# Attention's head mix on quarters of TensorE, with regroupings in halves issued from GpSimd

## The chip, the core and the metric

The kernel runs on one core of a Trainium2 chip. A core has five engines with a queue of instructions each: TensorE (PE, an array of 128 x 128 cells for matmuls), VectorE (DVE), ScalarE (ACT), GpSimd (POOL) and SyncE (SP, which only issues DMAs). PE writes to PSUM, a memory of eight banks of 128 partitions x 512 float32; DVE and ACT read the banks, POOL doesn't. The queues run side by side and wait for each other by semaphores; each is worked off in its order. The metric is the device time of one execution in microseconds (us); lower is better.

## What is computed

Three layers follow each other. The first is attention whose heads are mixed before and after the softmax; the change touches this layer alone. B = 4 batches, 12 heads, 448 positions, 64 numbers per head, all in float32:

```python
scores = scale * np.matmul(q, k.transpose(0, 1, 3, 2))
scores = np.einsum('bhij,hg->bgij', scores, w_pre)
scores = scores - np.max(scores, axis=-1, keepdims=True)
attn = np.exp(scores)
attn = attn / (np.sum(attn, axis=-1, keepdims=True) + 1e-09)
attn = np.einsum('bhij,hg->bgij', attn, w_post)
return np.matmul(attn, v).astype(np.float32)
```

Its output goes to a dense layer (`h = x @ w_in`, `g = h * cos(h)`, `g @ w_out`) and to a layer of eight experts; these make up the rest of the program.

## The kernel before, in words

Attention is `phase_a`. A batch's 448 query rows are cut into four tiles of 120, 120, 120 and 90 rows (`ROWS`; the last ones overlap), 16 tiles in all. For each tile:

- `q_prep` turns the tile's queries by transposes on PE (tile name qt) and splits them into a high and a low part (q_hi, q_lo), with the rows sorted by their place in a ten. `k_prep` does it for the keys once a batch (kt, k_hi, k_lo).
- `scores` makes two heads at a time (name s): three products each, the two heads on the upper and the lower half of the array's rows. ACT or DVE copies each head's scores from PSUM to SBUF (ss).
- `sort` regroups: a DMA for each head moves its 120 x 448 scores into the tile s2, where a partition is a pair of one of ten rows and a head (10 x 12 = 120 partitions), and column block c holds the c-th ten of rows. It is issued by SP or by POOL. These are the rows `s<-ss` (for the first tile `s<-am`, since the scores rest in a tile am there).
- `pre` mixes the heads of ten rows by one matmul (name pre): a matrix `kron_pre` of 120 x 120, in which `w_pre` stands once for each of ten rows, times a column block of s2. DVE takes the maximum of each row (`top`, name mz), ACT the exponential and its sum (`exp`, name e). Three such blocks are a group; there are 60 groups and 180 blocks.
- `fin` makes 1/sum and scales the second mixing matrix `kron_post` with it (`weigh`, name wc). `post` then multiplies e with wc (name po): for each of four column parts three matmuls into one bank, copied out to am.
- `av` multiplies am with v: three steps of 16 matmuls a tile, two heads on the left and the right half of the array's columns.

Next to this, `narrow` converts the weights of the dense layer, which lie in DRAM in a wider format: a load (raw), some DVE and ACT operations (cvt, nar), an integer addition on POOL (nar, L542) and a store, 64 times.

The order of all this is made by a planner (`Plan`): each operation has the engines that could do it with a duration, a due time and what it depends on, and `schedule` deals them out one by one. It also counts the buffers (`PLACES`: three PSUM banks for pre, two for post, three for the others). What it settles is written into the queues in that order. `half` says whether a matmul uses the array in halves, and `TURN` is what the planner charges for going over.

## Time and profile before

| | |
|---|---|
| time, median of 3 runs | 934.05 us (928.82 to 935.58) |
| profiled execution | 931.55 us; span of its instructions 929.8 us |
| busy in the span | PE 887.1, DVE 610.5, ACT 546.7, POOL 126.6 us |
| pre-mix on PE (L405) | 360 records (two for each of 180 matmuls), 13.6% of the chain of waits |
| posts on PE (L443) | 1440 records, 15.0% of the chain |
| regroupings | 74 + 18 + 7 issued by POOL, 70 + 18 + 5 by SP |

The profile is one execution, taken by the hardware. Each row tells of a group of instructions: the line, the engine, the operation, output<-input by the program's tile names, and sizes as partitions x elements. A float32 matmul is two records on PE. PE's ends are modelled, since its matmuls are pipelined, so the distance between two starts says more than one duration. "The chain" is the work that ended last, followed back from the end, from each step to what released it. The granted clock (PEclk) is the share of TensorE's full speed that it was given.

### The profile page before, as it was taken

The page shows a single profiled execution, that of the slowest core. Times are in us where ns is not written, and L with a number is a line of the kernel's source. Part 1 is how long each engine was busy: PE and PEld are TensorE (multiplying, and loading weights), DVE is VectorE, ACT ScalarE, POOL GpSimd, SP SyncE. Part 2 cuts the span into 40 slices and gives each one's busy share as a digit, 9 for nine tenths or more (in the row PEclk, how much of TensorE's full clock was granted, in tenths as well). Part 3 has the DMA queues.
Part 4 walks back from the last instruction along what each step waited for, and adds up shares of the span by engine and source line. Part 5 has one row for each costly group of instructions (what it writes and reads, how often), then busy time and mean ns, then how long its engine had stood idle before and what let it go on. Part 6 is the DMA issues. An engine that isn't in the chain of part 4 may idle for free.

```text
span 929.8 us, 17837 instructions
## 1 busy us (share of the span) xinstructions
PE 887.1 (95%) x6602; PEld 634.8 (68%) x6602; DVE 610.5 (66%) x1277; ACT 546.7 (59%) x1199; POOL 126.6 (14%) x184
## 2 busy tenths in 40 slices
PE   7879999999999999999999999999999999999765
PEld 5557777777777777777778777777777787853212
DVE  4658888789888798787654656666756667833003
ACT  5547768677766777676665555565646558622003
POOL 2122233222322122222200000000000000010000
PEclk9989999999999999999999999999999999999768
DMA  8999887998879987887437712354464339889998
GB/s 169 206 193 223 203 235 212 231 226 231 227 201 243 226 237 193 225 210 212 123 119 223 266 54 69 119 204 136 154 203 136 116 109 303 260 335 415 415 377 319
DMA packets 179622, 198.89 MB, mean 214 GB/s; under 512 B 70892, under 2 KB 154578, under 8 KB 179536
## 3 DMA queue, kind: packets, MB, share of 16 engines
q1 hardware_dynamic: 169404, 177.14, 64.3%
q0 software_dynamic: 7520, 19.98, 9.0%
q8 instruction: 52, 0.85, 0.4%
q10 hardware_dynamic: 2612, 0.65, 0.3%
q14 instruction: 34, 0.28, 0.1%
HBM read 135.40 MB, written 23.59 MB: 171 GB/s over the span
## 4 chain that ended last, share of the span: by engine, by line
PE 82%; DMA 11%; ACT 2%; SPq 2%; DVE 1%; issue 1%; ACTq 0%; DVEq 0%
PE po L443 15%; PE pre L405 14%; PE h L705 8%; PE av L467 8%; PE h L706 8%; PE h L708 8%; PE s L358 7%; DMA s<-ss 4%; DMA early<-in_moe_w_dram 3%; PE gt L745 3%; DMA ring<-in_moe_w_dram 2%; DMA cg<-in_moe_w_dram 2%; PE eh L1046 2%; PE lg L754 1%; PE p L817 1%; PE kt L292 1%
## 5 line engine op out<-in xcount | busy, mean ns | idle before, releaser
L443 PEld LDWEIGHTS po<-wc,e 120*112 120x112 f32 x1440 | 172.1, 177 | 60.1 <-issue 44.5
L443 PE MATMUL po<-wc,e 120*112 120x120 f32 x1440 | 183.6, 269 | 0.6 <-ACT am L228 0.6
L405 PE MATMUL pre<-s,kron_pre 120*120 120x448 f32 x360 | 166.2, 549 | 2.1 <-DMA s<-ss 1.7
L408 DVE TENSOR_REDUCE mz<-pre 120x1 f32<-120x448 f32 x180 | 111.3, 621 | 49.5 <-PE pre L405 47.8
L705 PE MATMUL h<-x,wh 128*128 128x512 f32 (+1 forms) x384 | 142.0, 380 | 0.7 <-ACT wh L649 0.7
L706 PE MATMUL h<-x,wh 128*128 128x512 f32 (+1 forms) x384 | 136.1, 364 | 0.0
L228 ACT COPY am<-po 112x360 f32<-112x360 f32 x189 | 87.3, 462 | 69.9 <-PE po L443 67.7
L412 ACT ACTIVATE e<-pre,mz 120x448 f32<-120x448 f32 x180 | 114.9, 639 | 21.1 <-DVE mz L408 19.0
L721 ACT ACTIVATE cg<-h,consts 128x512 f32<-128x512 f32 (+1 forms) x64 | 40.4, 632 | 88.2 <-PE h L708 86.9
L705 PEld LDWEIGHTS h<-x,wh 128*128 128x128 f32 x384 | 72.2, 188 | 24.1 <-ACT cg L721 8.0
L708 PE MATMUL h<-x,wf 128*128 128x512 f32 (+1 forms) x384 | 87.5, 363 | 0.0
L467 PE MATMUL av<-am,v 112*64 112x120 f32 (+1 forms) x1536 | 82.8, 262 | 0.7 <-ACT xst L228 0.7
L378 POOL DMA_DIRECT2D s<-ss x92 | 54.8, 596 | 207.4 <-ACT ss L228 107.3
L467 PEld LDWEIGHTS av<-am,v 112*64 112x64 f32 x1536 | 74.0, 137 | 11.2 <-issue 3.0
L542 POOL TENSOR_TENSOR nar<-nar,cvt 128x384 uint32<-128x384 uint32 x64 | 63.9, 999 | 117.2 <-DVE cvt L533 51.4
L706 PEld LDWEIGHTS h<-x,wh 128*128 128x128 f32 x384 | 72.3, 188 | 10.6
L722 DVE TENSOR_SCALAR cg<-cg 128x512 f32<-128x512 f32 (+1 forms) x64 | 25.1, 393 | 78.0 <-ACT cg L721 77.5
L708 PEld LDWEIGHTS h<-x,wf 128*128 128x128 f32 x384 | 66.2, 188 | 11.9
L228 ACT COPY ss<-s 120x448 f32<-120x448 f32 (+1 forms) x102 | 53.1, 532 | 27.9 <-PE s L358 12.5
L650 DVE TENSOR_TENSOR wf<-wf,wh 128x768 fp32r<-128x768 f32 x64 | 60.9, 952 | 11.1 <-ACT wh L649 11.1
L405 PEld LDWEIGHTS pre<-s,kron_pre 120*120 120x120 f32 x360 | 53.0, 184 | 15.5 <-issue 12.5
L226 DVE COPY ss<-s 120x448 f32<-120x448 f32 (+1 forms) x78 | 48.3, 620 | 18.9 <-PE s L358 17.8
(174 smaller groups left out, 1259.6 us busy)
## 6 DMA issues: line engine op xcount, KB each, us to landing
early<-in_moe_w_dram SPq DMA_DIRECT2D x36, 768.0 KB
wf<-w SPq DMA_DIRECT2D x64, 384.0 KB
s<-ss POOLq DMA_DIRECT2D x74, 210.0 KB, 6.4
s<-ss SPq DMA_DIRECT2D x70, 210.0 KB
raw<-in_moe_w_in_dram SPq DMA_DIRECT2D x32, 384.0 KB
w<-nar SPq DMA_DIRECT2D x64, 192.0 KB
raw<-in_moe_w_out_dram SPq DMA_DIRECT2D x32, 384.0 KB
gn<-in_moe_w_dram SPq DMA_DIRECT2D x16, 768.0 KB
```

Of the source, the lines that this page charges most:

```text
L228: nc.scalar.copy(out=out, in_=in_)
L358: nc.tensor.matmul(pts[o][:n, :S], x[r, p, :n], y[r, p, :], start=(i == 0), stop=(i == 2))
L405: nc.tensor.matmul(prt[gi, c][:, :S], kpre, s2t[ti][:, 3 * g + c, :], start=True, stop=True)
L408: nc.vector.tensor_reduce(out=mz[gi][:, 0, c:c + 1], in_=prt[gi, c][:, :S], axis=AX.X, op=ALU.max, negate=True)
L412: nc.scalar.activation(out=et[gi][:, c, :], in_=prt.pop((gi, c))[:, :S], func=AF.Exp, bias=mz[gi][:, 0, c:c + 1], accum_out=mz[gi][:, 1, c ...
L443: nc.tensor.matmul(pt[:, :360].rearrange("p (g i) -> p g i", i=30)[:, :, 10 * c:10 * c + 10], et[gi][:, c, jt * CJ:(jt + 1) * CJ], wct[gi] ...
L467: nc.tensor.matmul(pt[64 * o:64 * o + 64, x * 120:x * 120 + n], vt[:, g, jt, :], am[ti % 2][:, g, jt, :n], start=(jt == 0), stop=(jt == NJ ...
L542: nc.gpsimd.tensor_tensor(out=f, in0=f, in1=x["t"], op=ALU.add)
L650: nc.vector.tensor_tensor(out=wf_t[v], in0=wf_t[v].bitcast(F32), in1=wh.bitcast(F32), op=ALU.subtract)
L705: nc.tensor.matmul(pt, wh[:, c], xh[:, c, :], start=(c == 0), stop=False)
L706: nc.tensor.matmul(pt, wh[:, c], xl[:, c, :], start=False, stop=False)
L708: nc.tensor.matmul(pt, wl[:, c], xh[:, c, :], start=False, stop=(c == 5))
```

## The change

The pre-mix is done on quarters of the array. Query rows are grouped by five instead of ten, so a tile has 24 fives (20 for the last tile, which now has 100 rows instead of 90). s2 has 128 partitions: five rows x 12 heads from partition 0, and another five x 12 from partition 64 (r = 0, 1). `kron_pre` is 60 x 60 (in 64 columns), once in each half of the partitions. A step of `pre` is four matmuls: upper or lower half of the rows (r), left or right half of the columns (c), each with its own column block of s2. They fill two PSUM banks (one for each r) with 2 x 60 rows in 128 partitions. There are 92 such steps, in 44 groups of two and 4 groups of one; DVE takes 184 maxima and ACT 184 exponentials, over 128 partitions. A group's post has four matmuls (two in the groups of one) for each of four column parts, and its copy to am moves 480 columns (240).

`fin` is two operations for the planner, sum and reciprocal (`turn`) and the scaling (`weigh`), both on DVE as before.

Each head's regrouping is two DMAs of half its rows. For all tiles but the first they can be issued by POOL only; for the first by SP or POOL.

The buffers for e go from 3 of three blocks to 5 of two, mz gets four of its own, nar goes from 5 to 4. The planner tells rows, columns and quarters apart as ways of using the array. The loads of the last tile's queries are one DMA instead of two, its store to DRAM likewise.

```diff
-PLACES = {"pre": 3, "post": 2, "ps": 3, "knat": 2, "qnat": 2, "ssrc": 8, "s2": 2, "e": 3, "wc": 2, "xst": 1,
-          "raw": 4, "nar": 5, "cv_t": 3}
+PLACES = {"pre": 3, "post": 2, "ps": 3, "knat": 2, "qnat": 2, "ssrc": 8, "s2": 2, "e": 5, "mz": 4, "wc": 2,
+          "xst": 1, "raw": 4, "nar": 4, "cv_t": 3}
 SPARE = 3 * ["ps", "pre", "ps", "pre", "ps", "post", "pre", "post"]
...
-def build_kron(nc, pool, wb_pool, ident, w, scale, name, inner):
-
-    wb = wb_pool.tile([120, 12], F32, name=f"wb_{name}")
-    nc.scalar.dma_start(out=wb, in_=w.unsqueeze(0).to_broadcast([10, 12, 12]))
+def build_kron(nc, pool, ident, w, scale, name, cols):
+
+
+    wb = pool.tile([128, 12], F32, name=f"wb_{name}")
+    nc.vector.memset(wb, 0.0)
+    m = pool.tile([128, 2, 5], F32, name=f"m_{name}")
+    nc.vector.memset(m, 0.0)
+    for r in range(2):
+        p = slice(64 * r, 64 * r + 60)
+        nc.scalar.dma_start(out=wb[p], in_=w.unsqueeze(0).to_broadcast([5, 12, 12]))
+        nc.vector.tensor_reduce(out=m[p, r if cols == 10 else 0], in_=ident[p, p].rearrange("p (i h) -> p i h", i=5),
+                                axis=AX.X, op=ALU.add)
...
-    m = wb_pool.tile([120, 10], F32, name=f"m_{name}")
-    nc.vector.tensor_reduce(out=m, in_=ident[:120, :120].rearrange("p (i h) -> p i h", i=10),
-                            axis=AX.X, op=ALU.add)
-    kr = pool.tile([120, 120], F32, name=f"kron_{name}")
+    kr = pool.tile([128, 120 if cols == 10 else 64], F32, name=f"kron_{name}")
+    if cols == 10:
+        out = kr.rearrange("p (g i) -> p g i", i=10)
+    else:
+        nc.vector.memset(kr, 0.0)
+        out = kr[:, :60].rearrange("p (i g) -> p g i", i=5)
     nc.vector.tensor_tensor(
-        out=kr.rearrange("p (g i) -> p g i", i=10) if inner else kr.rearrange("p (i g) -> p g i", i=10),
-        in0=wb.unsqueeze(2).to_broadcast([120, 12, 10]),
-        in1=m.unsqueeze(1).to_broadcast([120, 12, 10]),
+        out=out,
+        in0=wb.unsqueeze(2).to_broadcast([128, 12, cols]),
+        in1=m.rearrange("p r i -> p (r i)")[:, :cols].unsqueeze(1).to_broadcast([128, 12, cols]),
...
-    ROWS = [120, 120, 120, 90]
-    NG = [4, 4, 4, 3]
+    ROWS = [120, 120, 120, 100]
+    ROW0 = [0, 120, 240, S - 100]
+    QUADS = [[2, 2, 2], [2, 2, 2], [2, 2, 2], [2, 2, 1]]
...
-        groups = [(ti, g) for ti, (b, t) in enumerate(tiles) for g in range(NG[t])]
-        NT, NGR = len(tiles), len(groups)
-        first = [groups.index((ti, 0)) for ti in range(NT)]
+        groups = [(ti, sum(QUADS[t][:g]), n) for ti, (b, t) in enumerate(tiles) for g, n in enumerate(QUADS[t])]
+        NT = len(tiles)
+        first = [groups.index((ti, 0, 2)) for ti in range(NT)] + [len(groups)]
+
+        at = [2 * sum(n for _, _, n in groups[:gi]) / 3 for gi in range(len(groups) + 1)]
...
+                nc.sync.dma_start(
+                    out=qnat[ti][:ROWS[t], h:h + m],
+                    in_=q[b, h:h + m, ROW0[t]:ROW0[t] + ROWS[t], :].rearrange("h i d -> i h d"))
+            qload[ti, part] = dma(0.5, 0.65, start, due=due, late=3.0 if ti > 1 else 0.0, takes=[qslot[ti]] if part == 0 else [],
...
-            def sort(o):
-                h = 2 * p + o
+            def sort(o, r):
+                h, m = 2 * p + o, n // 2
 
                 def f(e):
-                    if h == 0:
-                        s2t[ti] = room(sg, "s2", [120, 12, S], F32, f"s2_{ti}")
-                    QUEUE[e].dma_start(out=s2t[ti][h::12, :n // 10], in_=x[o][:n])
+                    if (h, r) == (0, 0):
+                        s2t[ti] = room(sg, "s2", [128, 12, S], F32, f"s2_{ti}")
+                    QUEUE[e].dma_start(out=s2t[ti][64 * r + h:64 * r + 60:12, :n // 10],
+                                       in_=x[o][m * r:m * r + m])
                 return f
...
-                sorted_[ti, h] = plan.op([("SP", 1.0), ("POOL", 0.8)], sort(o), [c], due,
-                                         takes=[] if h else [s2l[ti]], uses=ss + ([s2l[ti]] if h else []),
-                                         moves=1.0 * n / 120, behind=[sorted_[ti, 0]] if h else [])
...
+                for r in range(2):
+                    start = h == 0 and r == 0
+                    sorted_[ti, h, r] = plan.op([("POOL", 0.62)] if ti else [("SP", 0.55), ("POOL", 0.62)], sort(o, r), [c], due,
+                                                takes=[s2l[ti]] if start else [], uses=ss + ([] if start else [s2l[ti]]),
+                                                moves=0.5 * n / 120, behind=[] if start else [sorted_[ti, 0, 0]])
...
+        def pre(gi, x, due):
+
+
+            ti, q0, nq = groups[gi]
+            b = [Slot("pre") for _ in range(2)]
+            el[gi, x] = Slot("e")
+            if x == 0:
+                mzl[gi] = Slot("mz")
...
-                if c == 0:
-                    et[gi] = sl.tile([120, 3, S], F32, tag="e", name=f"e{gi}", bufs=PLACES["e"])
-                    mz[gi] = sl.tile([120, 3, 3], F32, tag="mz", name=f"mz{gi}", bufs=PLACES["e"])
-                prt[gi, c] = bank(b, f"pre{gi}_{c}")[:120]
-                nc.tensor.matmul(prt[gi, c][:, :S], kpre, s2t[ti][:, 3 * g + c, :], start=True, stop=True)
...
-            m = plan.op([("PE", 0.76)], mul,
-                        [sorted_[ti, h] for h in range(H)], due, behind=[mixed[gi]] if c else [],
-                        takes=[b] + ([el[gi]] if c == 0 else []), uses=[s2l[ti]] + ([] if c == 0 else [el[gi]]))
...
+                et[gi, x] = sl.tile([128, 2, S], F32, tag="e", name=f"e{gi}_{x}", bufs=PLACES["e"])
+                for r in range(2):
+                    prt[gi, x, r] = bank(b[r], f"pre{gi}_{x}_{r}")
+                for c in range(2):
+                    for r in range(2):
+                        nc.tensor.matmul(prt[gi, x, r][64 * c:64 * c + 64, :S], kpre[64 * r:64 * r + 60],
+                                         s2t[ti][64 * r:64 * r + 60, 2 * (q0 + x) + c, :], start=True, stop=True)
...
+            m = plan.op([("PE", 0.91)], mul, [sorted_[ti, h, r] for h in range(H) for r in range(2)], due,
+                        behind=[mixed[gi]] if x else [], takes=b + [el[gi, x]] + ([] if x else [mzl[gi]]),
+                        uses=[s2l[ti]] + ([mzl[gi]] if x else []), half="quarters")
...
-            x = plan.op([("DVE", 0.54)], top, [m], due, uses=[b, el[gi]])
-            expd[gi, c] = plan.op([("ACT", 0.63)], exp, [x], due, uses=[b, el[gi]])
+            for r in range(2):
+                t = plan.op([("DVE", 0.54)], top(r), [m], due, uses=[b[r], mzl[gi]])
+                expd[gi, x, r] = plan.op([("ACT", 0.63)], exp(r), [t], due, uses=[b[r], el[gi, x], mzl[gi]])
...
         def fin(gi, due):
+            nu = 2 * groups[gi][2]
             wcl[gi] = Slot("wc")
 
-            def weigh(e):
-                wct[gi] = sl.tile([120, 3, 120], F32, tag="wc", name=f"wc{gi}", bufs=PLACES["wc"])
-                z, rz = mz[gi][:, 1], mz[gi][:, 2]
+            def turn(e):
+                z, rz = mz[gi][:, 1, :nu], mz[gi][:, 2, :nu]
                 nc.vector.tensor_scalar(out=z, in0=z, scalar1=1e-9, scalar2=None, op0=ALU.add)
                 nc.vector.reciprocal(out=rz, in_=z)
-                nc.vector.tensor_tensor(
-                    out=wct[gi], in0=kpost.unsqueeze(1).to_broadcast([120, 3, 120]),
-                    in1=rz.unsqueeze(2).to_broadcast([120, 3, 120]), op=ALU.mult)
-            return plan.op([("DVE", 0.92)], weigh, [expd[gi, c] for c in range(3)], due,
-                           takes=[wcl[gi]], uses=[el[gi]])
+
+            def weigh(e):
+                wct[gi] = sl.tile([128, 4, 120], F32, tag="wc", name=f"wc{gi}", bufs=PLACES["wc"])
+                (nc.vector if e == "DVE" else nc.gpsimd).tensor_tensor(
+                    out=wct[gi][:, :nu], in0=kpost.unsqueeze(1).to_broadcast([128, nu, 120]),
+                    in1=mz[gi][:, 2, :nu].unsqueeze(2).to_broadcast([128, nu, 120]), op=ALU.mult)
+            t = plan.op([("DVE", 0.35)], turn, [expd[gi, x, r] for x in range(nu // 2) for r in range(2)], due,
+                        uses=[mzl[gi]])
+            return plan.op([("DVE", 0.06 + 0.13 * nu)], weigh, [t], due, takes=[wcl[gi]], uses=[mzl[gi]])
...
                 pt = made["po", gi, jt] = bank(b, f"po{gi}_{jt}")[:CJ]
-                for c in range(3):
-                    nc.tensor.matmul(
-                        pt[:, :360].rearrange("p (g i) -> p g i", i=30)[:, :, 10 * c:10 * c + 10],
-                        et[gi][:, c, jt * CJ:(jt + 1) * CJ], wct[gi][:, c, :], start=True, stop=True)
+                for x in range(nq):
+                    for r in range(2):
+                        u = nq * r + x
+                        nc.tensor.matmul(
+                            pt[:, :240 * nq].rearrange("p (g i) -> p g i", g=12)[:, :, 10 * u:10 * u + 10],
+                            et[gi, x][:, r, jt * CJ:(jt + 1) * CJ], wct[gi][:, u, :], start=True, stop=True)
 
             def out(e):
...
+            m = plan.op([("PE", 0.456 * nq)], mul, [f], due, takes=[b], uses=es + [wcl[gi]])
+            amdone[gi, jt] = plan.op([("ACT", 0.06 + 0.2 * nq), ("DVE", 0.1 + 0.24 * nq)], out,
+                                     [m] + ([avs[ti - 2, s] for s in range(3)] if ti > 1 else
+                                            [sorted_[0, h, r] for h in range(H) for r in range(2)] if ti else []),
+                                     due, uses=[b])
```

Where it moves instructions, at the same place of the program (the pre-mix of the seventh tile, s_6, while the scores of the eighth are made): PE's queue before, with the pre-mixes of single tens between posts (po) of the group before, transposes of keys (kt) and scores (s).

```order
L292 MATMUL kt_2_2483<-ident,knat_0_1945 128x112 x4
L405 MATMUL pre_0_2494<-s_6_2008,kron_pre 120x448
L443 MATMUL po_1_2505<-wc_2345,e_2233 112x12x10 x3
L443 MATMUL po_2_2510<-wc_2345,e_2233 112x12x10 x3
L405 MATMUL pre_1_2516<-s_6_2008,kron_pre 120x448
L443 MATMUL po_3_2520<-wc_2345,e_2233 112x12x10 x3
L358 MATMUL s_6_2525<-k_hi,q_hi 90x448
L358 MATMUL s_7_2526<-k_hi,q_hi 90x448
```

And PE's queue now, at the second group of that tile:

```order
L338 MATMUL qt_0_2659<-ident,qnat_2394 128x120 x2
L427 MATMUL pre_0_0_2670<-s_6_2071,kron_pre 64x448
L427 MATMUL pre_0_1_2671<-s_6_2071,kron_pre 64x448
L427 MATMUL pre_0_0_2670<-s_6_2071,kron_pre 64x448
L427 MATMUL pre_0_1_2671<-s_6_2071,kron_pre 64x448
L304 MATMUL kt_3_2682<-ident,knat_1_2300 128x112 x4
L371 MATMUL s_8_2689<-k_hi,q_hi 100x448
L371 MATMUL s_9_2690<-k_hi,q_hi 100x448
```

A step is four rows that write two banks (pre_0_0 and pre_0_1), and stands for two of the rows before; ahead of it and behind it the array is used in another way. Counted over the whole order, the way of using the array changes 212 times before and 320 times now.

POOL's queue before, where that tile is regrouped (s_6 is the tile s2, ss_0 to ss_10 are heads; the odd heads are issued by SP):

```order
L378 DMA s_6_2008<-ss_0_1969 10x12x448
L378 DMA s_6_2008<-ss_2_1998 10x12x448
L378 DMA s_6_2008<-ss_4_2098 10x12x448
L542 TENSOR_TENSOR nar_2102<-nar_2102,cvt_2074 128x384
L378 DMA s_6_2008<-ss_6_2125 10x12x448
L378 DMA s_6_2008<-ss_8_2202 10x12x448
L378 DMA s_6_2008<-ss_10_2262 10x12x448
```

And now:

```order
L391 DMA s_6_2071<-ss_0_2042 5x12x448 x2
L391 DMA s_6_2071<-ss_1_2046 5x12x448 x2
L584 TENSOR_TENSOR nar_1980<-nar_1980,cvt_1978 128x384
L391 DMA s_6_2071<-ss_2_2117 5x12x448 x2
L391 DMA s_6_2071<-ss_3_2119 5x12x448 x2
L584 TENSOR_TENSOR nar_2060<-nar_2060,cvt_2058 128x384
L391 DMA s_6_2071<-ss_4_2182 5x12x448 x2
L391 DMA s_6_2071<-ss_5_2184 5x12x448 x2
```

All twelve heads stand in this queue now, two issues each, with the additions of the weight conversion between them; SP's queue holds no regrouping behind the first tile's. The planner also dealt out the copies anew: of the 192 copies of scores DVE has 100 instead of 82, and ACT 92 instead of 110; of the am copies DVE has 64 of 192 instead of 51 of 240.

## Rows read from the trace of the kernel before

**Rows 1.** Windows: length, busy us (instructions) of PE, PEld, DVE, ACT, POOL; clock, DMA share, GB/s

```profile
0.00:100.00 100.00, 86.03 (x590) 59.65 (x590) 63.00 (x136) 59.95 (x146) 21.60 (x37) 0.97 0.94 202
100.00:450.00 350.00, 349.06 (x3016) 257.12 (x3016) 287.05 (x634) 247.69 (x636) 99.08 (x128) 1.00 0.85 219
```

**Rows 2.** Chain of work that ended last: start us, us, what

```profile
21.82 9.16 DMA s<-ss
...
57.85 10.75 DMA s<-ss
...
416.55 1.39 PE av L467 x32
```

**Rows 3.** Windows of the pre-mix's line L405 alone, PE and PEld

```profile
0.00:100.00 100.00, 27.77 (x62) 9.69 (x62) 0.97 0.94 202
100.00:450.00 350.00, 122.67 (x265) 38.37 (x264) 1.00 0.85 219
```

**Rows 4.** Timeline of PE near the stage's end: start us, us, what, records

```profile
457.09 1.86 PE L467 MATMUL av<-am,v 112*64 112x120 f32 x32
458.88 0.44 PE L358 MATMUL s<-k_hi,q_hi 64*90 64x448 f32 x2
...
459.66 0.87 PE L443 MATMUL po<-wc,e 120*112 120x120 f32 x6
460.36 0.92 PE L405 MATMUL pre<-s,kron_pre 120*120 120x448 f32 x2
461.12 0.78 PE L443 MATMUL po<-wc,e 120*112 120x120 f32 x6
461.73 0.92 PE L405 MATMUL pre<-s,kron_pre 120*120 120x448 f32 x2
...
499.93 0.50 PE L705 MATMUL h<-x,wh 128*128 128x512 f32 x1
```

**Rows 5.** Timeline of PE in the next stage

```profile
537.59 1.06 PE L754 MATMUL lg<-cg,wphi 128*32 128x512 f32 x8
538.59 0.50 PE L705 MATMUL h<-x,wh 128*128 128x512 f32 x1
```

**Rows 6.** Groups of DVE, 0 to 500 us: count, busy us, mean ns, idle before

```profile
L408 DVE TENSOR_REDUCE mz<-pre 120x1 f32<-120x448 f32 x180 | 111.3, 621 | 49.5 <-PE pre L405 47.8
L226 DVE COPY ss<-s 120x448 f32<-120x448 f32 (+1 forms) x78 | 48.3, 620 | 18.9 <-PE s L358 17.8 <-DMA raw<-in_moe_w_in_dram 0.8
...
L430 DVE TENSOR_TENSOR wc<-kron_post,mz 120x360 f32<-120x360 f32 x60 | 34.8, 579 | 2.1
...
L226 DVE COPY am<-po 112x360 f32<-112x360 f32 x51 | 27.0, 529 | 6.8 <-PE po L443 6.4
...
L428 DVE TENSOR_SCALAR mz<-mz 120x3 f32<-120x3 f32 x60 | 15.3, 254 | 6.8 <-ACT e L412 6.7
...
L429 DVE RECIPROCAL mz<-mz 120x3 f32<-120x3 f32 x60 | 10.7, 178 | 2.1
```

**Rows 7.** Timeline of DVE at a dense place

```profile
299.81 0.62 DVE L226 COPY ss<-s 120x448 f32<-120x448 f32 x1
300.34 0.61 DVE L408 TENSOR_REDUCE mz<-pre 120x1 f32<-120x448 f32 x1
```

**Rows 8.** Regroupings and POOL's additions: count, ns min/median/max; landing; group of L542

```profile
L378 POOL DMA_DIRECT2D s<-ss x92: 582/598/756, 21.1 to 460.6; - x92
...
L378 POOL DMA_DIRECT2D s<-am x7: 598/598/722, 11.7 to 17.9; - x7
...
DMA to landing us min/median/max: 2.6/6.1/10.9
...
L542 POOL TENSOR_TENSOR nar<-nar,cvt 128x384 uint32<-128x384 uint32 x64 | 63.9, 999 | 117.2 <-DVE cvt L533 51.4 <-DMA qnat<-in_q_dram 13.3 <-ACT e L412 12.8
```

**Rows 9.** Waits: who for whom, us in total, times, longest

```profile
POOL nar L542 <- DVE cvt L533: 51.4, 19, 9.4
```

**Rows 10.** Waits of PE from 100 to 450 us, the same columns

```profile
PE pre L405 <- DMA s<-ss: 0.2, 1, 0.2
```

More of the change, by code (lines that the diff above doesn't have):

```diff
@@ L337, in low @@
                 nc.vector.tensor_tensor(out=dst(ql), in0=src(), in1=dst(qh).bitcast(F32), op=ALU.subtract)
-            free = [qk[ti - 1, p] for p in (2 * x, 2 * x + 1)] if ti else []
+            free = []
+            if ti:
+                m = ROWS[tiles[ti - 1][1]]
+                free = [qk[ti - 1, p] for p in range(6) if p * m < 2 * n * (x + 1) and (p + 1) * m > 2 * n * x]
             idle = WARM[x] if ti == 1 else 0
@@ L447, in out @@
-            def out(e):
-                copy(e, am[ti % 2][:, :, jt, 30 * g:30 * g + 30],
-                     made["po", gi, jt][:, :360].rearrange("p (g i) -> p g i", i=30))
-            m = plan.op([("PE", 0.63)], mul, [f], due, takes=[b], uses=[el[gi], wcl[gi]])
-            amdone[gi, jt] = plan.op([("ACT", 0.36), ("DVE", 0.46)], out,
-                                     [m] + ([avs[ti - 2, s] for s in range(3)] if ti > 1 else [sorted_[0, h] for h in range(H)] if ti else []), due, uses=[b])
+                for x in range(nq):
+                    for r in range(2):
+                        u = nq * r + x
+                        nc.tensor.matmul(
+                            pt[:, :240 * nq].rearrange("p (g i) -> p g i", g=12)[:, :, 10 * u:10 * u + 10],
+                            et[gi, x][:, r, jt * CJ:(jt + 1) * CJ], wct[gi][:, u, :], start=True, stop=True)
@@ L455, in phase_a @@
         xst, xl = {}, {}
         def av_mul(ti, s, pt):
-            n = 30 * NG[tiles[ti][1]]
+            n = ROWS[tiles[ti][1]]
             if s == 0:
@@ L481, in store_x @@
             else:
-                queue.dma_start(out=xd[:, :, r0:r0 + 80], in_=xst[ti][:, :, :80])
-                queue.dma_start(out=xd[:, :, r0 + 80:r0 + 88], in_=xst[ti][:, :, 82:90])
+                queue.dma_start(out=xd[:, :, r0:r0 + 88], in_=xst[ti][:, :, 12:100])
         def av(ti, due):
@@ L488, in av @@
             outs = []
-            need = [amdone[first[ti] + g, jt] for g in range(NG[t]) for jt in range(NJ)]
+            need = [amdone[gi, jt] for gi in range(first[ti], first[ti + 1]) for jt in range(NJ)]
             for s in range(3):
```

85 lines of the change are left out of this document (43 added, 42 removed).

## The prediction

> **What bounds the kernel now.** Read the windows first [rows 1]. Attention is the first 500 us: then the next stage's first matmul (h) starts [rows 4]. From 100 to 450 us PE is busy 349.06 of 350 us, DVE 287, ACT 248, POOL 99, at the full clock: this stretch lasts as long as PE's own work. The first 100 us are different: PE is busy 86 us, the DMA share is 0.94, and three pieces of the chain, at 21.82, 32.00 and 57.85 us, are regroupings of 9 to 11 us that it waits for (first and last in [rows 2]). So work taken off PE shortens the stage fully in the middle and only partly at the start. Of the pre-mix's records 62 lie before 100 us and 265 in the middle [rows 3], the rest of the 360 after it.
>
> Then PE's order of time [rows 4], by the distance from one start to the next, since ends are modelled. A pre-mix takes 461.12 - 460.36 = 0.76. A post of three matmuls takes 461.73 - 461.12 = 0.61, so 0.205 for each. After a score the same post takes 460.36 - 459.66 = 0.70: leaving the halved array costs 0.09. A score pair takes 0.78; av takes 1.79 with 120 columns and 1.39 with 90 (chain, [rows 2]).
>
> **Part by part.**
>
> *Pre-mix.* Removed: 180 x 0.76 = 136.8 us. Added: 92 groups of four matmuls of 60 x 64, each on its own quarter. The trace has no quarters, so bounds: if the four stream side by side, a group needs one pre-mix's time, 0.76; if only two do, 1.52. The nearest row is lg in the next stage [rows 5]: four float32 matmuls on four column strips of the array, eight records, and the next instruction starts 1.00 us after the first. One full matmul of 512 columns would be 0.76 x 512/448 = 0.87; of the 0.13 left over 0.09 is a mode change and 0.04 the start of four. That rows run side by side too is seen in the scores, though in a shorter format: two records on half the rows each last 0.44 us together, two of the pre-mix 0.92 [rows 4]. I take 0.76 + 0.04 = 0.80 without mode changes: 92 x 0.80 = 73.6. Change: -63.2 us.
>
> *Mode changes.* PE's order holds 212 changes between full, row-halved and column-halved array before, and 320 of those and quarters after, since nearly every group stands alone between other work (the PE rows of the change show two). 108 x 0.09 = +9.7 us. The bounds are nothing (the drain hidden by the new group's start) and twice that.
>
> *Post, av, scores.* 736 post matmuls instead of 720: 16 x 0.205 = +3.3. The last tile of each batch has 100 rows instead of 90: 12 av steps x 0.40 x 10/30 = +1.6. Scores stream 448 columns whatever the rows: 0.
>
> Sum on PE: -63.2 + 9.7 + 3.3 + 1.6 = -48.6 us. By the shares of [rows 3] 73.6% of it is in the middle (-35.8), 17.2% at the start (-8.4), 9.2% at the end (-4.4).
>
> The Trainium skill, "TensorE: Matmul & The Clock Gate", Part 3, section "Measured speedup vs the span model", gives a speedup of 3.07 and not 4 for four row tiles. By that figure a group is an estimated 4 x 0.76 / 3.07 = 0.99 us instead of 0.80, and the sum -31 us. lg's 1.00 us, for 512 columns and with a mode change in it, speaks for the smaller price.
>
> *DVE and ACT.* The order gives the counts, [rows 6] the durations. 184 maxima for 180 (4 x 0.62 = +2.5 us); score copies on DVE 100 for 82 (18 x 0.62 = +11.2); 64 am copies for 51, most of 480 columns instead of 360 (0.53 x 1.2 = 0.64 each, so 41 for 27: +14); 25 more small copies of q and xst, at most 0.53 each (+13). 48 rounds of sum, reciprocal and weighting for 60, the weighting a third longer: 60 x 1.01 = 60.7 becomes 48 x (0.43 + 0.77) = 57.6 (-3). Together +38 on DVE; ACT loses the same copies and has room. In the middle DVE goes from 287 to about 287 + 0.74 x 38 = 315 us, of a stretch that shrinks to 314. That looks full, but busy time overstates it: two DVE instructions of 0.62 and 0.61 us start 0.53 us apart [rows 7], so a DVE that is never idle does 1.16 times its busy time, and the real load is near 315/1.16 = 272 of 314. It hides behind PE, with less cover than today; I charge 3 us of new waits.
>
> *GpSimd.* Regroupings are now halves, 384 in all, 372 of them on POOL instead of 99. Its issue takes 0.60 us for a whole and hardly varies (582 to 756 ns) [rows 8]. A half can cost anything down to nothing; I take 0.60, since the first tile's issues of 90 rows (s<-am) are as long as those of 120. 372 x 0.60 + 64 weight additions (nar) x 1.0 = 287 us in a stage of 460: 62% of POOL, or 14.4 + 4.3 = 19 us of each tile's 29. It is hidden as long as each issue is early enough for its tile. The first tile's issues share SP and POOL; twelve more of them cost the start about 1 us, inside the waits for loads there. SP loses 88 issues and its loads go earlier. The three long regroupings of the chain were issued by SP, behind loads; they could get shorter, which I count as nothing, because the DMA share there is 0.94 whoever issues. The 6.1 us median to landing [rows 8] I keep: the bytes in flight are the same.
>
> *Constants.* Four small DMAs instead of two on ACT and seven more small DVE instructions ahead of the first transposes: 0, hidden by the loads of k; without that cover about 1 us.
>
> **Sum.** Middle -35.8, end -4.4, start half of 8.4 (-4.2), new waits +3: -41.4. The profiled execution took 931.55 us (span 929.8), 2.5 under the median of three, 934.05, and inside their spread of 928.82 to 935.58. 931.55 - 41.4 = **890 us**. The rest of the program, from 500 us on, is untouched and moves up as a whole.
>
> **Rivals.**
>
> *DVE sets the pace* (20%). For it: 315 of 314 us by its busy time; maxima and weightings are in the path of every group, and only three pre-mix banks serve groups that take two. Against it: the overlap of 1.16. If DVE fills to 93% by busy time, the middle lasts 315/0.93 = 339 instead of 314: +25, less the 3 charged, 912 us.
>
> *POOL is late* (8%). Its queue is in order, a weight addition has waited up to 9.4 us for DVE [rows 9], and now all halves of a tile stand behind it. 2 us of PE waiting on each of 15 tiles is +30: 920 us. Against it: POOL has a third of its time free, and PE waits for regroupings 0.2 us in the whole middle [rows 10].
>
> *GpSimd's issues stall behind DVE* (2%). If each of 372 issues waited out one DVE operation of 0.62 us [rows 7], POOL would need 287 + 231 = 518 us for the stage and be its bound: 931.55 - 500 + 518 = 950 us. But 92 issues beside a DVE that is busy 82% of the time never passed 756 ns [rows 8]. The Trainium skill, "SBUF — State Buffer", section "SBUF: two separate sides", warns of this for the DVE operations that take the shared ports; the row just named does not bear it out here.
>
> *Only two quarters at a time* (6%), the other side. A group is then 1.52: 92 x 1.52 - 136.8 = +3.0, with mode changes, post and av +17.6; no new waits. 931.55 + 17.6 = 949 us. It decides from 92c = 136.8 - 14.6, a group of c = 1.33 us. Four strips in 1.00 speak against it.
>
> *More than forecast* (9%): regroupings leave SP's backlog and the three stalls of about 30 us shrink by a third: -10, 880 us.
>
> **How the numbers follow.** The forecast has 55%, its own range is 880 to 900 (mode changes at nothing or twice). The range for 8 in 10 goes down to the better start with a little of the mode changes' bound, 876, and up to the DVE case and the lower half of the POOL case, 916. Left out are the pair case and the upper POOL and the stall cases. About 1%, 9 us, is what a measurement of this kernel can tell from no change. Faster by over 1%: forecast, better start, DVE case and most POOL cases, 0.88. Within 1%: 0.05. Slower: the pair case and the stalls, 0.07.
>
> **What would show it.** Right: pre records in fours that start within some 20 ns, and the next matmul about 0.89 us after a lone group; the first h matmul near 459 us instead of 500; PE still busy 97% or more from 100 us to the last tiles; POOL issues of 0.60 us. Wrong: quarters that start one after another; PE idle before pre-mixes released by regroupings (POOL late) or before posts released by DVE's weighting (DVE). An error of more than 15 us would come from waits, not from matmul times.

## The result and the profile after

The changed kernel takes 946.2 us (943.9 to 948.6, four runs) where the kernel before takes 933.2 beside it: 1.0133 times as long, 95% interval 1.0101 to 1.0164. It is slower by 1.3%, where 890 us were forecast. The profiled execution took 948.59 us (span 946.8), 17.0 more than that of before; the next stage's first matmul comes 17.8 us later, so all of it was lost in attention.

The windows of the kernel after, with the columns of [rows 1]:

```profile
0.00:100.00 100.00, 75.91 (x582) 50.25 (x586) 57.19 (x125) 47.49 (x112) 45.88 (x81) 0.93 0.95 169
100.00:450.00 350.00, 327.66 (x3179) 228.21 (x3172) 312.84 (x638) 218.43 (x550) 214.39 (x327) 0.99 1.00 222
```

PE, busy 349.06 us of the middle before, now idles for 22 of 350; DVE went from 287 to 313, POOL from 99 to 214, and the DMA share from 0.85 to 1.00 at the same 220 GB/s. PE's timeline shows the quarters, and the end of the stage, which answers to [rows 4]:

```profile
314.42 0.98 PE L427 MATMUL pre<-s,kron_pre 60*64 60x448 f32 x8
315.33 1.89 PE L482 MATMUL po<-wc,e 128*112 128x120 f32 x16
...
517.77 0.50 PE L748 MATMUL h<-x,wh 128*128 128x512 f32 x1
```

A group of four quarter matmuls takes 0.91 us with its change of mode, as forecast (0.89), but h starts at 517.77 instead of 499.93. The longest pieces of transfers in the chain of the kernel after (start, us, what), one at the start and four in the middle:

```profile
30.25 9.97 DMA s<-am
...
206.42 8.99 DMA s<-ss
...
303.66 17.54 DMA v<-in_v_dram
321.21 18.35 DMA knat<-in_k_dram
...
430.36 9.03 DMA s<-ss
```

The first pre-mix waits for a regrouping of the first tile (s<-am) until 40.36 us, 13.6 later than before. In the middle, from 100 to 450 us, the regroupings (s<-ss) hold 12.7% of the chain, 44 us, against 2.4%, 8 us, in the kernel before; GpSimd's issues of them hold 5.4%, 19 us, and the loads of v and k 18 us each. PE's waits from 0 to 520 us name no single culprit: the largest sum, for loads of queries, is 6.8 us, and the next named one, for DVE's weighting, 5.7.

To place the losses, this table gives the start of av, from PE's timeline, for the second and the fourteenth tile: up to the second tile's counts as the start of the program, the distance between the two as its middle. The column us is the median; the others are from one profiled execution, which lies up to 6 us from it (e5).

| kernel | us | 2nd tile | 14th tile | distance | first h |
|---|---|---|---|---|---|
| before | 933.2 | 100.2 | 457.1 | 356.9 | 499.9 |
| after | 946.2 | 111.1 | 478.4 | 367.3 | 517.8 |
| e4 before, halves from GpSimd | 953.4 | 109.1 | 487.7 | 378.6 | 527.4 |
| e7 before, whole from GpSimd | 933.3 | 101.6 | 463.9 | 362.3 | 501.8 |
| e5 quarters, whole, both queues | 918.8 | 109.7 | 454.5 | 344.8 | 493.4 |
| e6 quarters, whole, GpSimd | 926.6 | 101.1 | 456.4 | 355.3 | 495.7 |
| e8 after, no conversion | 941.6 | 124.0 | 471.0 | 347.0 | 509.9 |
| e9 e5, no conversion | 903.4 | 101.8 | 433.1 | 331.3 | 471.9 |
| e16 after, no conversion or its loads | 907.6 | 106.4 | 437.3 | 330.9 | 476.7 |
| e17 e6, no conversion or its loads | 894.8 | 90.9 | 420.9 | 330.0 | 460.3 |
| e18 before, no conversion or its loads | 925.1 | 96.2 | 451.6 | 355.4 | 494.5 |

The change lost 10.9 us at the start and 10.4 in the middle, where 33 were to be won, and won 3.5 at the end.

### The profile page after: what moved, and what is told of

Same layout as the page of the kernel before. It is cut to its first block, busy times and chain, and to the rows that moved or that the text cites. A ratio compares the mean times of both kernels' runs of the same rounds, so it can differ in the third digit from the quotient of the medians.

```text
span 946.8 us, 18806 instructions
## 1 busy us (share of the span) xinstructions
PE 872.6 (92%) x7010; PEld 606.8 (64%) x7010; DVE 650.4 (69%) x1308; ACT 514.8 (54%) x1103; POOL 285.2 (30%) x457
## 4 chain that ended last, share of the span: by engine, by line
PE 58%; DMA 19%; DVE 10%; SPq 4%; issue 3%; POOL 3%; ACT 3%; ACTq 0%; DVEq 0%; POOLq 0%
PE po L482 9%; PE h L748 8%; PE h L749 8%; PE h L751 8%; PE av L510 5%; DMA s<-ss 5%; PE pre L427 4%; PE s L371 4%; DMA early<-in_moe_w_dram 4%; PE gt L788 3%; DMA knat<-in_k_dram 2%; DVE mz L434 2%; POOL s L391 2%; DMA v<-in_v_dram 2%; DMA cg<-in_moe_w_dram 2%
## 5 line engine op out<-in xcount | busy, mean ns | idle before, releaser
L391 POOL DMA_DIRECT2D s<-ss x360 | 211.1, 591 | 145.9 <-ACT ss L241 38.3
L482 PEld LDWEIGHTS po<-wc,e 128*112 128x112 f32 x1472 | 159.9, 178 | 48.2 <-issue 16.6
L482 PE MATMUL po<-wc,e 128*112 128x120 f32 x1472 | 178.2, 273 | 11.3 <-DVE wc L465 5.7
L442 ACT ACTIVATE e<-pre,mz 128x448 f32<-128x448 f32 x184 | 115.4, 632 | 106.9 <-DVE mz L434 106.9
L434 DVE TENSOR_REDUCE mz<-pre 128x1 f32<-128x448 f32 x184 | 105.8, 615 | 38.9 <-PE pre L427 38.8
L427 PE MATMUL pre<-s,kron_pre 60*64 60x448 f32 x736 | 108.8, 574 | 16.0 <-issue 6.1
L510 PE MATMUL av<-am,v 112*64 112x120 f32 (+1 forms) x1536 | 85.3, 266 | 1.0 <-ACT xst L241 1.0
L241 ACT COPY am<-po 112x480 f32<-112x480 f32 (+1 forms) x128 | 69.2, 546 | 27.2 <-PE po L482 26.6
L584 POOL TENSOR_TENSOR nar<-nar,cvt 128x384 uint32<-128x384 uint32 x64 | 64.1, 1008 | 38.2 <-ACT nar L580 9.8
L239 DVE COPY ss<-s 120x448 f32<-120x448 f32 (+1 forms) x96 | 57.9, 615 | 10.2 <-PE s L371 10.2
L241 ACT COPY ss<-s 120x448 f32<-120x448 f32 (+1 forms) x84 | 44.1, 535 | 25.5 <-PE s L371 12.9
```

The source lines that it names most:

```text
L241: nc.scalar.copy(out=out, in_=in_)
L391: QUEUE[e].dma_start(out=s2t[ti][64 * r + h:64 * r + 60:12, :n // 10], in_=x[o][m * r:m * r + m])
L427: nc.tensor.matmul(prt[gi, x, r][64 * c:64 * c + 64, :S], kpre[64 * r:64 * r + 60], s2t[ti][64 * r:64 * r + 60, 2 * (q0 + x) + c, :], star ...
L434: nc.vector.tensor_reduce(out=mz[gi][:, 0, u:u + 1], in_=prt[gi, x, r][:, :S], axis=AX.X, op=ALU.max, negate=True)
L442: nc.scalar.activation(out=et[gi, x][:, r, :], in_=prt.pop((gi, x, r))[:, :S], func=AF.Exp, bias=mz[gi][:, 0, u:u + 1], accum_out=mz[gi][: ...
L482: nc.tensor.matmul(pt[:, :240 * nq].rearrange("p (g i) -> p g i", g=12)[:, :, 10 * u:10 * u + 10], et[gi, x][:, r, jt * CJ:(jt + 1) * CJ], ...
```

## The experiments

The theories at first: GpSimd's issues (they stretch DVE and stand in one queue), DVE's own load, the constants at the start, and a wrong price of the quarters.

**e1, both queues.** The regroupings of every tile on SP and GpSimd:

```
-[("POOL", 0.62)] if ti else [("SP", 0.55), ("POOL", 0.62)]
+[("SP", 0.55), ("POOL", 0.62)]
```

> The changed kernel, with the regroupings of every tile dealt out to SP and GpSimd (some 178 and 169 issues of a half head) instead of 372 on GpSimd. The changed kernel took 946 us; from the av of its second tile (111.1 us) to that of its fourteenth (478.4) it needs 367 us, with PE idle for some 36 of 350 us. GpSimd theory (its issues stretch DVE's instructions, and its queue and its transfers land late): half of that goes, 367 falls to 335-350 us and the time to 914-930 us; DVE's conversion instructions beside a DMA issue are as long one by one, but there are half as many. DVE theory (DVE has simply too much to do, who issues does not matter): 367 stays within 5 us, the time is 941-951. Theory of the start: nothing changes before 111 us in both cases, since the first tile was dealt out to both already.

Measured: 987.3 us, ratio to before 1.057 (1.053 to 1.062). Neither theory. (In the changed kernel PE idles for 22 of 350 us, by its window above, and not for 36.) The middle of e1, columns as above, and the row of SP's issues (count, ns min/median/max, first and last start):

```profile
100.00:450.00 350.00, 312.42 (x2939) 219.49 (x2939) 275.38 (x576) 201.21 (x510) 121.49 (x171) 0.93 0.78 204
...
L391 SPq DMA_DIRECT2D s<-ss x187: 712/738/4466, 33.6 to 517.6; - x187
```

A half costs SP 738 ns; before, a whole head took it 785 (median of 88). SP's queue carries the loads of q, k, v and weights as well, and twice the issues are likely to delay them. The DMA share is only 0.78 here, so full DMA engines are not what this kernel loses by; the regroupings hold 22.2% of its chain in the middle. Halving doubles the price on whichever queue issues it, and GpSimd, with room to spare, was the better of the two.

**e2, constants.** Zero fills and sums first, scaling and products on GpSimd:

```
-    nc.vector.tensor_scalar(out=wb, in0=wb, scalar1=scale, scalar2=None, op0=ALU.mult)
+    nc.gpsimd.tensor_scalar(out=wb, in0=wb, scalar1=scale, scalar2=None, op0=ALU.mult)
```

> The changed kernel, with the building of the two constants put in another order: all zero fills and small sums first, so that ACT can issue its four small DMAs at once, and the scaling and the two products on GpSimd instead of DVE. In the changed kernel ACT's first cast starts at 9.67 us (4.30 before) and the second score at 13.09 us. If the constants hold up the start: ACT's first cast at 4.5-5.5 us, scores at 9.5-10.5 us, the first pre-mix at 35-38 instead of 40.36, and 2-5 us off the time: 941-944 us. If that delay is hidden by the loads of the second tile and by the regroupings behind it: the first pre-mix stays within 1 us of 40.4 and the time within 2 of 946.

Measured: 945.0 us (1.0114, 1.0080 to 1.0149); the scores start at 10.2 us (the second matmul at 10.9 instead of 13.1), the first pre-mix at 38.2. The constants cost about 2 us of the start and the time does not tell them from nothing. ACT's first cast still came at 9.25 us: its third small DMA waits, in the program, for its first to land.

**e3, a dearer pre-mix.** Each matmul writes all 128 columns, with a constant of that width, and the planner is told 1.61 us for a group instead of 0.91:

```
-prt[gi, x, r][64 * c:64 * c + 64, :S], kpre[64 * r:64 * r + 60]
+prt[gi, x, r][:, :S], kpre[64 * r:64 * r + 60]
```

> The changed kernel, but each of the four matmuls of a group writes all 128 columns of its bank, the second of a bank over what the first wrote, so that only two can run side by side (half of the pre-mix's result is lost by that). A group should last about 1.6 us instead of 0.91: 92 x 0.7 = 64 us more work on PE. If PE sets the pace of the changed kernel, the time goes to 1000-1012 us. If something else sets the pace in the stage's middle and PE waits there (some 36 us from 100 to 450 us, and as much at the start), the waits take up much of it: 955-985 us.

Measured: 987.0 us, 41 more than after. PE's timeline:

```profile
301.63 1.77 PE L427 MATMUL pre<-s,kron_pre 60*128 60x448 f32 x8
303.33 0.42 PE L338 MATMUL qt<-ident,qnat 120*128 120x120 f32 x2
```

A group takes 1.70 us, so PE has 92 x 0.79 = 73 us more work, of which 32 vanished in waits. It lies between the two expectations: PE is still near the bound, but no longer the bound.

**e4 and e7, the regroupings alone.** The kernel before with halves as in the changed kernel (e4), and with whole heads, `[("POOL", 0.8)] if ti else [("SP", 1.0), ("POOL", 0.8)]` (e7):

> The kernel before (whole-array pre-mix, old groups), with its regroupings alone made as in the changed kernel: in halves of a head, from GpSimd for all tiles but the first, SP and GpSimd for the first. GpSimd theory: its 372 issues stretch DVE's instructions and its transfers land late, which costs here too: 945-970 us against 932, and conversion instructions of up to 2.4 us beside an issue. DVE theory (it is the copies and maxima that DVE was given): the regroupings cost nothing but at the start, 932-940 us.

> The kernel before, with its whole-head regroupings issued from GpSimd alone behind the first tile. With halves from GpSimd alone it took 953 against 934. If the halving costs: 930-938 us. If GpSimd alone costs: 945-955.

Measured: halves 953.4 us (1.0209, 1.0161 to 1.0258), whole heads from GpSimd 933.3 (0.9987, 0.9958 to 1.0016). So GpSimd as the only issuer costs the kernel before nothing that the interval shows, and the halving costs 20 us. The rows of the queue and of the issues, first e4 (queue: packets, MB, share; issue: count, KB, median us to landing):

```profile
q0 software_dynamic: 28416, 37.95, 19.0%
...
s<-ss POOLq DMA_DIRECT2D x288, 105.0 KB, 7.6
```

and e7:

```profile
q0 software_dynamic: 14272, 37.96, 17.9%
...
s<-ss POOLq DMA_DIRECT2D x144, 210.0 KB, 7.6
```

The same bytes take twice the packets, each half as large, and half a head needs the same 7.6 us to land as a whole one. The engines' own time for these packets hardly grows: 19.0% of a span of 956.6 us against 17.9% of 931.1, or 9%. In the chain from 100 to 450 us the regroupings hold 10.1% in e4, some 35 us, and none in e7, at DMA shares of 0.92 and 0.88.

**e5 and e6, quarters with whole heads.** The heads' rows stand 13 partitions apart, so one stride crosses both halves of the array:

```
-QUEUE[e].dma_start(out=s2t[ti][64 * r + h:64 * r + 60:12, :n // 10], in_=x[o][m * r:m * r + m])
+QUEUE[e].dma_start(out=s2t[ti][h:128:13, :m], in_=x[o][:m * len(range(h, 128, 13))])
```

> The quarters of the changed kernel, but a head is regrouped by one transfer again: the heads' rows stand 13 partitions apart instead of 12, so that one stride runs through both halves of the array (the last head needs a second, small transfer; eight unused partitions are zeroed once at the start, and the pre-mix's constant is laid out to match and built on GpSimd). 13 transfers a tile instead of 24, dealt out to SP and GpSimd as in the kernel before. If the halving is what costs (384 issues that are each as long as one of a whole head, and as many transfers): the 20 us that the halves cost in the kernel before come back, and more where they meet a full DVE: 905-925 us against 946. If it is GpSimd's or DVE's load whoever carries the heads: 935-948.

> As the kernel with quarters and whole heads, but with GpSimd alone issuing behind the first tile (195 issues instead of 372). If the halving costs: within 8 us of that kernel, below 930. If it is that everything stands in GpSimd's one queue and its issues slow DVE: 12-25 us above that kernel.

Measured: 918.8 us on both queues (0.9835, 0.9797 to 0.9873) and 926.6 from GpSimd alone (0.9939, 0.9913 to 0.9965). The expectation of the halving held: 20 to 27 us came back (about 2 of them by the constants, which e5 and e6 build as e2 does), and the first pre-mix starts at 29 us. Of that GpSimd alone gives away 8, at the edge of what e6 allowed for the halving. The middle of e5, columns as above:

```profile
100.00:450.00 350.00, 335.66 (x3374) 241.10 (x3367) 313.28 (x667) 224.92 (x567) 108.39 (x143) 0.99 0.85 224
```

The DMA share is that of before; DVE is as full as in the changed kernel.

**e13, GpSimd's time.** e6, with 0.6 us of zero fills on GpSimd ahead of every whole-head issue:

```
+if e == "POOL" and not r:
+    [nc.gpsimd.memset(idle_p, 0.0) for _ in range(2)]
```

> The kernel with whole heads from GpSimd alone (927 us), with two zero fills of a small unused tile (about 0.3 us each) on GpSimd ahead of each whole-head issue, so that each regrouping takes GpSimd's queue some 1.2 us, as two halves do, while the transfers stay whole. If the halves cost by the time and the lateness of GpSimd's queue: 940-950 us, as the changed kernel. If they cost by the number and size of the transfers: 925-932.

Measured: 930.4 us, 4 above e6. Its middle has the changed kernel's DVE and POOL, to within 10%, but not its DMA share:

```profile
100.00:450.00 350.00, 328.76 (x3288) 234.82 (x3286) 313.77 (x641) 224.94 (x563) 233.16 (x487) 0.99 0.88 220
```

DVE's conversion steps are held beside GpSimd as well, the slowest for 2.45 us, where the changed kernel has 2.58. So neither the time on GpSimd's queue nor DVE stretched by GpSimd makes up the 20 us: together they come to 4, and the intervals of e6 and e13 overlap. The transfers' number and size are left.

**e8 and e9, DVE's load.** The changed kernel (e8) and e5 (e9) without the conversion's steps on DVE and GpSimd (`size`, `least`, `shift`, `sign`, `plus` of `narrow`):

> The changed kernel without DVE's and GpSimd's part of the weight conversion (the four cvt instructions of each of 64 pieces and the addition nar; ACT's part, the loads and the stores stay, so the weights of the next stage are wrong). DVE loses 64 x (3 x 0.35 + 0.55) = 102 us of busy time and what GpSimd's issues add to it, GpSimd 64 us. If DVE sets the pace of the middle: PE's waits there go and the time falls by 25-40 us to 906-921. If the regroupings' own way (issue, queue, landing) sets it: 935-946.

> The kernel of quarters with whole heads (919 us), without DVE's and GpSimd's part of the weight conversion (four cvt instructions of each of 64 pieces and the addition nar; the weights of the next stage are wrong). DVE loses 102 us of 408 in the first 500 us. With the halves gone, DVE is the next suspect for the 29 us between 919 and the 890 forecast: PE waits 8.4 us for its weighting and DVE is busy 47.8 of 50 us from 100 to 200 us. If DVE sets the pace there: 890-903 us. If the waits come from the three pre-mix banks, of which a group takes two, or from loads: 910-920.

Measured: 941.6 us and 903.4. With halves that is 5 us, with whole heads 15: DVE was the next bound behind the halves (the edit also takes 64 additions off GpSimd). By the table DVE's relief shortens the middle in e8 as well, by 20 us, and the start gave back 13 of them: with another order, made by the planner, the second tile's av comes at 124.0 us. In its chain a load of k holds the path from 98.1 us for 14.6; why it comes so late was not followed up. Every edit here makes the planner deal out anew, so that differences of a few us hold some of its order too.

**e16, e17 and e18, the other loads.** Without the conversion and its 64 loads of 384 KB; zeros are stored:

```
-ld = dma(0.45, 1.45, load, due=due - 1.5, late=6.0, takes=[raws], behind=behind)
...
-dma(0.4, 0.75, store, late=6.0, deps=[f], due=due + 1, uses=[fs])
+dma(0.4, 0.75, store, late=6.0, due=due + 1, behind=behind)
```

> The changed kernel without the weight conversion and without its 64 loads of 384 KB; its 64 stores stay and write zeros (the weights of the next stage are wrong). Without the conversion but with these loads it took 942. If the halves cost because the DMA engines are full: share in the middle from 1.00 to 0.75-0.85, the time to 905-920, and 8 us or less above the same with whole heads. If the halves cost in another way (more waits of their own): 930-942, and about 20 us above whole heads as with the loads.

> The kernel with whole heads from GpSimd alone (927 us), without the conversion and its loads as in the run before (zeros are stored). It loses DVE's 102 us of conversion too, which was worth 15 us with whole heads: 898-912 us in either case; what is looked for is the distance between these two.

> The kernel before without the weight conversion and its loads; its 64 stores stay and write zeros (the weights of the next stage are wrong). It is what the run of 894.75 us (quarters, whole heads, the same left out) is to be compared with. By the traces PE's work from the second tile's av to the fourteenth's is 356 us before and 329 us with quarters; if PE sets the pace of both, this one takes 920-932 us and the distance to 894.75 is 27-36 us, which is what quarters alone are worth. If the conversion and its loads slow the kernel before as well: 905-915 us, and the quarters are worth only 10-20.

Measured: 907.6, 894.8 and 925.1 us. The middles of e16 and e17:

```profile
100.00:450.00 350.00, 345.69 (x3596) 250.70 (x3597) 236.47 (x480) 207.24 (x525) 170.54 (x298) 1.00 0.67 162
```

```profile
100.00:450.00 350.00, 345.90 (x3614) 251.21 (x3611) 237.10 (x486) 205.18 (x521) 88.98 (x155) 1.00 0.64 166
```

Here halves and whole heads run alike, 330.9 and 330.0 us of middle, PE busy 99%. With loads and conversion they differ by 12.0 (after and e6), and e8, which leaves out the steps and keeps the loads, still needed 347.0: the middle's loss from the halves needs the conversion's loads. That it comes of full DMA engines (a share of 1.00 in the changed kernel, 0.67 in e16) is the likely reading and not shown by itself: without the loads SP's queue has 64 issues less too, and e4 loses as much at a share of 0.92. (These runs also take ACT's 64 conversions away, but ACT was busy 218 of 350 us.) The 13 us that remain between e16 and e17 lie at the start, 106.4 against 90.9 (some 2 us of it by the constants). From 10 to 40 us the share is 0.27, 0.76 and 0.87 in e16's three tens of us, against 0.75, 0.98 and 1.09 in e17: there it is no matter of full engines, and the issues are what differs. The row of the changed kernel:

```profile
L391 SPq DMA_DIRECT2D s<-am x12: 732/733/1801, 14.7 to 30.3; - x12
```

SP issues the first tile's halves from 14.7 to 31 us, in turn with the next tile's q; before, five whole heads were out by 18.8. And e18 against e17 says what the quarters are worth when nothing else is in the way: 30.3 us.

**e10, e11, e12, e14, e15, on the way to a better kernel.** From e5: all am copies on ACT (e10); banks for pre-mix, post and the rest dealt 4, 2, 2 (e11) and 4, 1, 3 (e12) instead of 3, 2, 3; e10 with the conversion's first step on ACT too (e14); and e14 with idle transposes ahead of the first groups (e15):

```
-[("ACT", 0.06 + 0.2 * nq), ("DVE", 0.1 + 0.24 * nq)], out
+[("ACT", 0.06 + 0.2 * nq)], out
...
+for _ in range(FILL[x] if gi < 2 else 0):
+    nc.tensor.transpose(prt[gi, x, 0][:, :128], ident, ident)
```

> The kernel of quarters with whole heads, with all copies of the mixed scores (am) on ACT; DVE loses about 64 x 0.64 = 41 us in the stage, ACT, busy 308 of 500 us, takes them. If DVE sets the pace: 900-912 us. If it does not, or if a copy that must now wait for ACT holds the post banks: 917-928.

> The kernel of quarters with whole heads, with four pre-mix banks instead of three and two instead of three for scores and transposes (two for post as before). At the start, where nothing else hides it, a group follows the one before after 3.24 us, because it needs two of three banks and the bank is free only after maximum and exponential. If that loop holds up the stage: the first post comes at 36-39 us instead of 42.6 and the time falls to 900-912. If the banks are not what is waited for: 917-935, the more the shorter supply of score banks hurts.

> As the kernel before this, but the fourth pre-mix bank is taken from post (one left). If the loop over three banks holds up the stage and post can do with one: 900-912 us. If post with one bank waits for each copy (0.66 us for one step of 0.9-1.8 us of PE): 960 or more, and then this says nothing on the pre-mix banks.

> Quarters with whole heads, all am copies on ACT (914 us), and the conversion's first step (the absolute value, dealt out to DVE and ACT before) on ACT alone too; DVE loses some 46 x 0.35 = 16 us more. If DVE still sets the pace: 905-912 us. If ACT has become as full: 912-920.

> As the kernel before this, with idle transposes ahead of the first four pre-mix groups (10, 8, 10 and 8), as the kernel has them ahead of the second tile's queries. Between 30 and 45 us PE ran at half its clock in the kernel with whole heads, after it had waited from 27 to 33 us. If that lower clock costs at the start: the clock from 30 to 45 us rises above 0.8, the first post comes 3-6 us earlier and the time falls by as much. If the start is bound by transfers and by the loop over three banks: within 3 us.

Measured: 914.0, 943.5, 929.0, 913.0 and 908.8 us. Moving 41 us off DVE gave 5 (the intervals of e5 and e10 overlap), less than was expected of a DVE that sets the pace alone, and e14 is not told apart from e10. e11 and e12 are worse than e5. In e12 PE waits 17 us for post's copies out of its one bank; in both the first post starts 3 us earlier than in e5 (39.8 and 39.4 us instead of 42.6), so the fourth bank helps at the start, and the banks' share of e5's waits in the middle stays open. e15's median is 4 us below e14's, and their intervals overlap. The windows from 30 to 45 us of e14 and of e15:

```profile
30.00:45.00 15.00, 11.69 (x39) 3.13 (x38) 5.54 (x11) 4.97 (x14) 1.71 (x3) 0.50 0.85 184
```

```profile
30.00:45.00 15.00, 14.18 (x105) 8.89 (x106) 10.21 (x21) 8.68 (x24) 1.71 (x3) 1.00 1.00 213
```

PE waited 2.0 us from 22.3 us on in e14, and the granted clock was 0.50, the lower of its two levels, 1.2 of 2.4 GHz, for all of these 15 us (0.54 in e5, after waits between 27 and 33 us). With the waits filled it stayed at 1.00 and the first post came at 39.24 us instead of 45.27. e15 is the fastest with the whole computation: 0.9752 of before (0.9721 to 0.9784), 37 us below the changed kernel.

## Why the prediction was wrong, step by step

**The pre-mix** was right in its mechanism: the four quarters of a group start within 20 ns (the median of the groups). The size was short: the second pass of a group starts 427 ns after the first, where a whole-array pass takes 378, so a group takes 0.85 us and not 0.80. The rival of two quarters at a time fell; e3 made it come true and measured it at 1.70 us. The estimate from the Trainium skill, "TensorE: Matmul & The Clock Gate", Part 3, section "Measured speedup vs the span model", 0.99 us, was too high.

**The PE sum** was too large. Between second and fourteenth tile PE is busy for 356.0 us before and 327.1 in e17 (not the 329 of e18's expectation): 28.8 less, where 12 of 16 tiles should give 36.5. By kind, from start to start without pauses: pre-mix -41.7, post +8.2, av +1.5, scores and transposes +3.1. 3.5 us of the 7.7 missing are the 0.05 of each of 70 groups; if the rest is mode changes (168 before, 251 in e17, in these tiles), one costs near 0.14 us and not 0.09. That is worked out, not measured by itself. e18 against e17 gives the whole as 30.3 us, where 41.4 were forecast with 3 us of waits.

**GpSimd** is the step that failed. That 372 issues of 0.6 us are hidden was nearly right (584 ns, [rows 8] has 598; e13 puts the time on the queue at 4 us). What was wrong is the 6.1 us to landing, kept because "the bytes in flight are the same": they are, but in twice as many transfers, and half a head needs as long to land as a whole one. The changed kernel's row, to be read beside the landings of [rows 8]:

```profile
s<-ss POOLq DMA_DIRECT2D x288, 105.0 KB, 8.2
```

So the regroupings, which the forecast had off PE's path, came late for their tiles: they hold 44 us of the chain in the middle, some 35 in e4, and none in e6 and e7. Halving costs 20 us, before (e4 against e7) and after (against e6). Meanwhile the DMA share rose to 1.00, and the loads of q, k and v came late as well. The share was in [rows 1]; it was used for the start alone. The Trainium skill, "DMA: Bandwidth & Descriptors", section "Anatomy of one DMA — SWDGE (gpsimd) path", splits a transfer into a fixed part of about 2.0 us and its bytes at 436 GB/s, so that halving saves little; e4 and e7 agree in kind, with 7.6 us for half and whole on a loaded system.

**The first tile** was put at 1 us "inside the waits for loads". It is the other half of the failure: the first pre-mix came 13.6 us late, some 2 us of it by the constants (put at 0), the rest most likely by SP's queue, in which a half costs as much as a whole, ahead of the loads.

**DVE** at 3 us was too little: e9 wins 15 us from it, and its rival, 912 us, is near to what remained without halves (918.8). The overlap factor of 1.16 from one dense place [rows 7] was taken for the whole middle. That three banks for groups of two, named in the rival, leave DVE no slack to be late in is argued; no run shows it for the middle.

**The rivals** each had one cause with the others hidden. POOL late (920) came nearest to what the halves did, but the regroupings were late in landing more than in POOL's queue (e13). GpSimd stalled behind DVE (950) is near the time and fell all the same: no issue took over 949 ns. The sum of the pieces, between kernels and each rounded: quarters -30 (e18 to e17), DVE and loads on whole heads +23 (what e6's -7 leaves of it), halves +20 (e6 to after): +13. The second piece is a remainder, so that the sum comes out by its making and proves nothing.

## What to carry to other kernels

When a layout forces a transfer to be cut in two, count both halves as whole transfers, on the queue that issues them and in the time to landing (on the DMA engines twice the packets took 9% more time here), and look at the DMA share of the stretch before calling them hidden: here it stood at 0.85 before the change. It can be cheaper to look for a layout that keeps the transfer whole: a stride of 13 instead of 12 gave some 20 us back. And work taken off the bound engine is paid out only as far as the next one: here DVE, busy 287 of 350 us, stood right behind PE.

## What was not expected of the hardware

GpSimd and DVE do get in each other's way, but in the other direction than the rival had it: GpSimd's issues stay short (949 ns at most), and some of DVE's conversion steps are held. A row of one of these steps in the kernel after, one of its instances on DVE's timeline, and what GpSimd did beside it:

```profile
L572 DVE TENSOR_SCALAR cvt<-cvt x64: 341/360/2579, 74.6 to 463.4; 128x384 uint32<-128x384 uint32 x64
...
299.74 2.58 DVE L572 TENSOR_SCALAR cvt<-cvt 128x384 uint32<-128x384 uint32 x1
...
300.14 1.96 POOL L584 TENSOR_TENSOR nar<-nar,cvt 128x384 uint32<-128x384 uint32 x2
```

2.58 us for an instruction of 0.36, which ends 0.2 us after two of GpSimd's additions. The additions are what holds DVE, not the issues: in the stage 122 conversion steps run beside issues alone, none of them more than 0.1 us over its usual time, and each of the 27 that last over 0.15 us longer runs beside an addition. The kernel before has 14 of these, all beside additions too. Maxima and copies of scores out of PSUM showed nothing of the kind (592 to 626 ns). The Trainium skill, "SBUF — State Buffer", section "SBUF: two separate sides", calls the shared ports a lock that the first comer keeps for its whole instruction; the trace agrees in that 25 of the 27 end after the addition, and not in who came first, since 13 of them had started before it, beside an issue. By e13 all this costs the kernel at most a few us.

The second is the clock: with more waits in the first 100 us the granted clock there was 0.93 instead of 0.97 [rows 1]. e15, which kept PE busy, had 1.00 where e14 had 0.50, with 4 us less in the median.
